# Linear attention in front of two feed-forward layers: the attention part rebuilt on row halves and column tiles of TensorE

## The chip, the cores and the metric

One NeuronCore of a Trainium2 chip runs the whole program. The metric is the device time of one execution in microseconds (us), median over runs. TensorE does the matmuls, VectorE (DVE) and ScalarE (ACT) work on 128 lanes, GpSimd (POOL) multiplies and issues some transfers, SyncE (SP) issues most transfers.

## The reference

Inputs q, k and v have 4 batches, 8 heads, 576 positions and 64 values; w_phi is 64x128. Everything is float32, with weights that arrive as float64.

```
def phi(x):
    proj = x @ w_phi                                   # 128 features
    proj = proj - max(abs(proj), axis=-1)
    return concatenate([exp(proj), exp(-proj)])        # 256 features
q_p, k_p = phi(q), phi(k)
kv, z = k_p.T @ v, sum(k_p over positions)             # 256x64 and 256 per head
x = (q_p @ kv) / (q_p @ z + 1e-6)                      # heads side by side: 2304 x 512
y = (sigmoid(x @ w_gate) * (x @ w_val)) @ w_out        # d_ff 1536
g = y @ w_in;  out = max(0.01 * g, g) @ w_out2         # d_ff 2048
```

## The kernel before

Attention works on 16 pairs of heads: 4 batches times 4 pairs, 128 lanes for the two heads' 64 values. Of the 576 positions 512 are "main" and 64 are the remainder; the remainders of two pairs are worked together. For one pair the steps are: transposes of k and q (`transposed`, tile `ps_t`), projection by a block-diagonal weight `wbd` of 128x256 that serves both heads at once (`proj`, tile `ps_p`), on VectorE the largest absolute value and the subtraction, on ScalarE the two exponentials (`ka`), the sum of features times values (`kv_main`, tile `kv`, 64 output lanes at a time), transposes of the centred q (`q_f`, tile `ps_q`) with their exponentials, and the weighted sums (`num`, tile `ps_n`). The weight of `num` is 128 columns wide: 64 columns are a head's values and one of the others is z, so the denominators come out as one more row of the same matmul. Then `norm1` to `norm3`: a DMA brings the denominator row onto 128 lanes, VectorE inverts it, two DMAs spread it through DRAM, POOL multiplies, and ScalarE and VectorE split the result x into a high part `xh` and a low part `xl`.

The feed-forward layers multiply such high and low parts in a format called float32r: `mm3` (lines 52 to 54) makes three matmuls, high by high, high by low and low by high. Before the change attention does so too in most pairs: `PLAIN_P` and `PLAIN_N` (line 254) name the pairs that use plain float32, 2 of 16 for the projection and 8 of 16 for the weighted sums. A plain float32 matmul stands in the trace as two matmul instructions, a float32r one as one. The split costs a ScalarE cast (line 48) and a VectorE subtraction (line 49; line 433 for the exponentials of q).

The weights are decoded from float64 on VectorE and ScalarE in pieces (`decode`, lines 102 to 114). While attention runs, the three decoded keys of the first feed-forward step are made, in 6 slots, and from pair 4 on `M` pieces put the first feed-forward step of batches 0 to 2 (tiles `pg`, `pv`, `po`) between the pairs. `ORDERS` and `SLOTS` say in which order the pieces of each pair are written; within that, a scheduler orders the instructions on every engine. PSUM has eight banks of 128x512: three shared ones (`at`), two for `kv` and `ps_n`, three for the feed-forward step. After attention come the rest of layer 1 and layer 2 (tile `ps_u` for the first matmul of each, `ps_p` again for the second), which the change does not touch.

Of the kernel before, what the change touches and what calls it, by code (L numbers as in the profile page):

```python
# [9 lines left out]
F32 = mybir.dt.float32  # L10
# [9 lines left out]
def linear_attention_moe(ctx, tc, q, k, v, w_phi, w_gate, w_val, w_out, w_in2, w_out2, out):  # L20
# [9 lines left out]
    NB = B + 1  # L30
    bw = [MAIN] * B + [REM * B]
# [4 lines left out]
    wpa = ctx.enter_context(tc.tile_pool(name="wpa", bufs=1))  # L36
    dr = ctx.enter_context(tc.tile_pool(name="dr", bufs=1, space=bass.MemoryType.DRAM))
# [33 lines left out]
    free = deque((wpa, f"w{i}") for i in range(6))  # L71
# [11 lines left out]
    pools = {}  # L83
# [44 lines left out]
    def first_weights():  # L128

        for i in range(3):  # L130
            _, w, expo = weight(1, 0, i)
            r = {k: take(F32R) for k in ("hi", "lo")}
            raws = [fetch((1, 0, i), j) for j in range(2)]
            yield
            for j, raw in enumerate(raws):
                cs = slice(512 * j, 512 * j + 512)
                m = pools["dec"].tile([128, 512], I32, tag="m", name="m")
                for n, _ in enumerate(decode(raw, m, r["hi"][0][:, cs], r["lo"][0][:, cs], expo)):
                    if n in (2, 4, 5):
                        yield  # L140
            for k in ("hi", "lo"):
                r["v" + k] = r[k][0].rearrange("p (k f) -> p k f", f=w)
            wts[1, 0, i] = r

    def decoded(keys, reserve, hold):
# [4 lines left out]
        for n, key in enumerate(keys):  # L150
# [34 lines left out]
            wts[key] = r  # L185

# [48 lines left out]
    def down1(c, b, h):  # L235
        for e in range(KD):
            po = pools["po"].tile([128, 512], F32, tag="po", name="po")[:, :bw[b]]
            for f in range(CH):
                if f:
                    yield 0  # L240
                mm_down1(po, wts[1, c, 2], b, e, h, f)
            first_sum(b, e, po, pools["tp"].tile([128, 512], F32, tag="st", name="st"))
            yield
# [10 lines left out]
    PLAIN_P, PLAIN_N = {0, 2}, {0, 1, 2, 3, 4, 5, 12, 14}  # L254

    wbd = wk.tile([128, 2 * NF], F32, name="wbd")
    wbh = wk.tile([128, 2 * NF], F32R, name="wbh")
    wbl = wk.tile([128, 2 * NF], F32R, name="wbl")
    nc.vector.memset(wbd, 0.0)

    ps = ps_a.tile([128, 128], F32, tag="at", name="ps_w", bufs=3)
# [13 lines left out]
    kvzs = {}  # L275
    for nm, dts in (("f", (F32,)), ("r", (F32R, F32R))):
        kvzs[nm] = []
        for i in range(1):
            z = [wk.tile([128, 2, 256], dt, name=f"kvz{nm}{i}{j}") for j, dt in enumerate(dts)]
            for t in z:  # L280
                if nm == "f":
                    nc.gpsimd.memset(t[:, :, 65:128], 0.0)
                else:
                    nc.gpsimd.tensor_copy(t[:, :, 65:128], kvzs["f"][i][0][:, :, 65:128])
            kvzs[nm].append(z)

    nat = {}

    def load_pair(b, c):
        for nm, src in (("k", k), ("q", q)):  # L290
            t = ld.tile([128, J, 2, D], F32, tag=nm, name=nm)
            for h in range(2):
                nc.sync.dma_start(out=t[:, :, h], in_=src[b, 2 * c + h, 0:MAIN, :].rearrange("(p j) d -> p j d", j=J))
            nat[nm, b, c] = t
            if (nm, b, c) == ("k", 0, 0):
                for h in range(2):
                    nc.sync.dma_start(out=wbd[64 * h:64 * h + 64, h * NF:(h + 1) * NF], in_=w_phi)
# [9 lines left out]
        vf = nat["v", b, c] = vfs[c % 2]  # L307
        for h in range(2):
            vs = v[b, 2 * c + h]
            nc.sync.dma_start(out=vf[:, 0:J, 65 * h:65 * h + 64], in_=vs[0:MAIN].rearrange("(p j) d -> p j d", j=J))  # L310
            nc.sync.dma_start(out=vf[64 * h:64 * h + 64, J, 66 * h:66 * h + 64], in_=vs[MAIN:S])

    def parts(ps, n, tag, b, c):

        if KD * b + c in PLAIN_P:
            x = xt.tile([128, n], F32, tag=tag + "hi", name=tag + "f")
            nc.scalar.copy(x, ps)
            return (x,)
        hi = xt.tile([128, n], F32R, tag=tag + "hi", name=tag + "hi")
        lo = xt.tile([128, n], F32R, tag=tag + "lo", name=tag + "lo")  # L320
        split(ps, hi, lo)
        return hi, lo

    def transposed(nm, b, c):
        src = nat.pop((nm, b, c))
        ps = ps_a.tile([128, 512], F32, tag="at", name="ps_t", bufs=3)
        for j in range(J):
            nc.tensor.transpose(ps[:, 128 * j:128 * j + 128], src[:, j].rearrange("p h d -> p (h d)"), ident)
        return parts(ps, MAIN, "x", b, c)

    def transposed_rem(nm, b, g):
        src = nat.pop((nm + "r", b, g))
        ps = ps_a.tile([128, 512], F32, tag="at", name="ps_t", bufs=3)
        nc.tensor.transpose(ps[:, 0:128], src.rearrange("p h d -> p (h d)"), ident)
        return parts(ps[:, 0:128], 128, "xr", b, 2 * g)

    def proj(x, c0, n, tag, bufs):

        ps = ps_a.tile([128, 2, 2, NF], F32, tag="at", name="ps_p", bufs=3)
        for i in range(n):  # L340
            l = [p[:, c0 + 128 * i:c0 + 128 * i + 128] for p in x]
            if len(l) == 1:
                nc.tensor.matmul(ps[:, i], l[0], wbd, start=True, stop=True)
            else:
                mm3(ps[:, i], l[0], l[1], wbh, wbl, True, True)
        m = wk.tile([128, 2, 2], F32, tag="m", name="m", bufs=4)
        nc.vector.tensor_reduce(out=m[:, :n], in_=ps[:, :n], axis=AX.X, op=ALU.max, apply_absolute_value=True)
        t = wk.tile([128, n, 2, NF], F32, tag=tag, name=tag, bufs=bufs)
        nc.vector.tensor_tensor(out=t, in0=ps[:, :n], in1=m[:, :n].unsqueeze(3).to_broadcast([128, n, 2, NF]), op=ALU.subtract)
        return t  # L350

    def features(t, n, tag, bufs):

        a = wk.tile([128, n, 2, 2, NF], F32, tag=tag, name=tag, bufs=bufs)
        for s, sc in enumerate((1.0, -1.0)):
            nc.scalar.activation(out=a[:, :, :, s, :], in_=t, func=ACTF.Exp, scale=sc)
        return a
# [6 lines left out]
    def t_k(p):  # L364
        p.kT = transposed("k", p.b, p.c)

    def t_q(p):
        p.qT = transposed("q", p.b, p.c)

    def t_r(p):  # L370
        if p.c % 2 == 0:
            rem["kT"] = transposed_rem("k", p.b, p.c // 2)
            rem["qT"] = transposed_rem("q", p.b, p.c // 2)

    def p_k(p, i):
        p.kf.append(features(proj(p.kT, 256 * i, 2, "t", 4), 2, "ka", 3))

    def p_kr(p):
        if p.c % 2 == 0:
            rem["k"] = features(proj(rem["kT"], 0, 1, "tr", 1), 1, "kar", 1)  # L380

    def p_q(p, i):
        p.tq.append(proj(p.qT, 256 * i, 2, "tq", 2))

    def p_qr(p):
        if p.c % 2 == 0:
            rem["q"] = proj(rem["qT"], 0, 1, "tqr", 1)

    def kv_main(p, s):

        ps = ps_a.tile([128, 2, 65], F32, tag=f"kv{s}", name="kv")
        vf = nat["v", p.b, p.c]
        cols = [slice(64 * i, 64 * i + 64) for i in range(2)]
        for j in range(J):
            for h in range(2):
                for cs in cols:
                    nc.tensor.matmul(ps[cs, h], p.kf[j // 2][:, j % 2, h, s, cs], vf[:, j, 64 * h:64 * h + 65], start=(h, j) == (0, 0), stop=False)
        for cs in cols:
            nc.tensor.matmul(ps[cs].rearrange("p h w -> p (h w)"), rem["k"][:, 0, p.c % 2, s, cs], vf[:, J], start=False, stop=True)
# [652 lines left out]
```

## Time and profile before

| | |
|---|---|
| Median of 3 runs | 1060.35 us (1058.79 to 1060.79) |
| The profiled execution's own time | 1053.95 us |
| Its span, first to last instruction | 1052.1 us |
| TensorE matmul busy | 1011.1 us, 96% |
| TensorE weight load busy | 843.9 us, 80% |
| VectorE busy | 778.9 us, 74% |
| ScalarE busy | 521.0 us, 50% |
| GpSimd busy | 169.7 us, 16% |
| Granted TensorE clock, mean | 0.995 |

Busy time counts a matmul from its start to a modelled end, and matmuls overlap, so a busy TensorE can still have room. How fast it works is read from the distance between the starts of successive matmuls.

### The profile page before, as it was taken

How to read it: one execution, taken by the hardware profiler on the slowest of the kernel's cores; microseconds unless marked ns; L12 is line 12 of the kernel's file. 1: busy time of each engine (PE TensorE's matmuls, PEld its weight loads, DVE VectorE, ACT ScalarE, POOL GpSimd, SP SyncE). 2: the span in 40 equal slices, each digit the busy share in tenths (PEclk: the TensorE clock that was granted, in tenths of full speed). 3: DMA queues.
4: the chain of work that ended last, by engine and by line, in shares of the span. 5: the costliest groups of instructions: out<-in, count | busy, mean ns of one | idle time of the engine just before them, and what ended most of it. 6: DMA issues, size and time to landing. Idle time of an engine off the chain costs nothing.

```text
span 1052.1 us, 16161 instructions
## 1 busy us (share of the span) xinstructions
PE 1011.1 (96%) x5986; PEld 843.9 (80%) x5986; DVE 778.9 (74%) x1373; ACT 521.0 (50%) x1066; POOL 169.7 (16%) x217
## 2 busy tenths in 40 slices
PE   7898999999999899999999999899999999999998
PEld 5677878788788788888888878688888888888886
DVE  4974877877389758395784969998797887979555
ACT  4666676767455545354454434487343343533221
POOL 0112121212201123324143120001010010101000
PEclk9999999999999999999999999999999999999999
DMA  5643344342298988769399494536172442515143
GB/s 142 156 101 89 95 102 108 79 109 75 69 304 243 314 162 257 96 151 268 62 251 189 88 322 180 179 132 239 41 240 82 159 156 85 183 58 180 43 165 132
DMA packets 119485, 160.13 MB, mean 152 GB/s; under 512 B 68720, under 2 KB 71408, under 8 KB 119408
## 3 DMA queue, kind: packets, MB, share of 16 engines
q1 hardware_dynamic: 95216, 94.09, 29.0%
q0 software_dynamic: 24192, 65.02, 24.4%
q8 instruction: 47, 0.77, 0.3%
q14 instruction: 30, 0.25, 0.1%
HBM read 109.64 MB, written 49.36 MB: 151 GB/s over the span
## 4 chain that ended last, share of the span: by engine, by line
PE 56%; DVE 6%; issue 5%; DMA 3%; POOL 2%; ACT 0%; POOLq 0%; ACTq 0%; DVEq 0%
PE ps_u L53 10%; PE ps_u L54 10%; PE ps_u L52 10%; PE ps_p L52 9%; PE ps_p L53 9%; PE ps_p L54 9%; POOL accd L682 2%; DVE acc L742 1%; DMA raw<-in_moe_w_gate_dram 1%; DVE w L753 1%; DMA w<-td 1%; DVE w L114 1%; DMA raw<-in_moe_w_out_dram 1%; POOL w L794 0%; DVE m L107 0%
## 5 line engine op out<-in xcount | busy, mean ns | idle before, releaser
L834 DVE TENSOR_TENSOR q<-ps_u,q 128x512 f32<-128x512 f32 x160 | 109.6, 686 | 66.6 <-PE ps_u L54 60.6
L52 PE MATMUL ps_u<-xh,w 128*128 128x512 f32 (+1 forms) x432 | 151.6, 352 | 1.6 <-ACT xh L48 1.5
L53 PE MATMUL ps_u<-xl,w 128*128 128x512 f32 (+1 forms) x432 | 152.1, 352 | 0.4 <-DVE xl L49 0.2
L54 PE MATMUL ps_u<-xh,w 128*128 128x512 f32 (+1 forms) x432 | 151.4, 351 | 0.0
L904 DVE TENSOR_TENSOR acc<-acc,ps_p 128x512 f32<-128x512 f32 x126 | 86.2, 684 | 39.5 <-PE ps_p L54 39.0
L52 PE MATMUL ps_p<-w,gh 128*128 128x512 f32 x288 | 112.2, 390 | 0.0
L53 PE MATMUL ps_p<-w,gh 128*128 128x512 f32 x288 | 112.0, 389 | 0.0
L54 PE MATMUL ps_p<-w,gl 128*128 128x512 f32 x288 | 111.8, 389 | 0.0
L794 POOL DMA_DIRECT2D w<-td x88 | 48.7, 563 | 379.9 <-PE ps_u L54 365.4
L682 POOL DMA_DIRECT2D accd<-w x80 | 70.7, 888 | 227.8 <-ACT w L681 141.9
L52 PE MATMUL ps_u<-w 128*128 128x512 f32 x256 | 100.1, 391 | 0.8 <-DVE q L834 0.8
L53 PE MATMUL ps_u<-w 128*128 128x512 f32 x256 | 100.0, 390 | 0.7 <-DMA w<-td 0.7
L54 PE MATMUL ps_u<-w 128*128 128x512 f32 x256 | 99.6, 389 | 0.0
L52 PEld LDWEIGHTS ps_u<-xh,w 128*128 128x128 f32 x432 | 82.2, 191 | 13.6 <-ACT xh L48 1.9
L53 PEld LDWEIGHTS ps_u<-xl,w 128*128 128x128 f32 x432 | 82.4, 191 | 12.3 <-DVE xl L689 0.6
L54 PEld LDWEIGHTS ps_u<-xh,w 128*128 128x128 f32 x432 | 82.2, 190 | 10.8
L470 POOL TENSOR_TENSOR rb<-u,rb 64x576 f32<-64x576 f32 x32 | 48.9, 1527 | 233.2 <-DMA rb<-rd 82.7
L52 PE MATMUL ps_p<-gh,w 128*128 128x512 f32 (+1 forms) x216 | 79.0, 370 | 7.6 <-DVE acc L685 4.1
L720 ACT ACTIVATE q<-q 128x512 f32<-128x512 f32 x48 | 30.2, 632 | 112.2 <-DVE q L834 112.1
L53 PE MATMUL ps_p<-gl,w 128*128 128x512 f32 (+1 forms) x216 | 79.8, 370 | 0.7 <-DVE gl L49 0.6
L54 PE MATMUL ps_p<-gh,w 128*128 128x512 f32 (+1 forms) x216 | 79.4, 369 | 0.0
L49 DVE TENSOR_TENSOR gl<-q,gh 128x512 fp32r<-128x512 f32 (+1 forms) x102 | 61.7, 613 | 19.3 <-ACT gh L48 19.1
(151 smaller groups left out, 2248.0 us busy)
## 6 DMA issues: line engine op xcount, KB each, us to landing
w<-td POOLq DMA_DIRECT2D x88, 512.0 KB, 6.1
td<-w SPq DMA_DIRECT2D x32, 512.0 KB, 3.3
accd<-w POOLq DMA_DIRECT2D x64, 256.0 KB, 6.1
raw<-in_moe_w_out_dram SPq DMA_DIRECT2D x28, 512.0 KB, 4.5
raw<-in_moe_w_in_dram SPq DMA_DIRECT2D x16, 512.0 KB, 4.2
raw<-in_moe_w_gate_dram SPq DMA_DIRECT2D x12, 512.0 KB, 5.4
raw<-in_moe_w_val_dram SPq DMA_DIRECT2D x12, 512.0 KB, 5.8
rb<-rd SPq DMA_DIRECT2D x32, 144.0 KB, 3.1
```

Source lines behind the costliest of these rows:

```text
L49: nc.vector.tensor_tensor(out=lo, in0=src, in1=hi.bitcast(F32), op=ALU.subtract)
L52: nc.tensor.matmul(ps, lh, rh, start=first, stop=False, **kw)
L53: nc.tensor.matmul(ps, lh, rl, start=False, stop=False, **kw)
L54: nc.tensor.matmul(ps, ll, rh, start=False, stop=last, **kw)
L114: nc.vector.tensor_tensor(out=lo, in0=mf, in1=hi.bitcast(F32), op=ALU.subtract)
L470: nc.gpsimd.tensor_tensor(out=p.rb[sl], in0=p.u[h][sl], in1=p.rb[sl], op=ALU.mult)
L682: nc.gpsimd.dma_start(out=accd[b][:, e], in_=st, accum_op=ALU.add)
L720: nc.scalar.activation(out=th, in_=t, func=ACTF.Lrelu)
L742: nc.vector.tensor_tensor(out=o, in0=x, in1=y, op=ALU.subtract)
L794: nc.gpsimd.dma_start(out=ts[n][k][0].bitcast(F32), in_=td[l, pair, n][:, k])
L834: nc.vector.tensor_tensor(out=o, in0=x, in1=y, op=ALU.add)
L904: nc.vector.tensor_tensor(out=a, in0=a, in1=po, op=ALU.add)
```

## The change

- The projection reads one head's 64 lanes and writes its 128 features: a matmul on a row half of TensorE (64 of 128 rows), 8 for k and 8 for q of a pair, with head 0 and head 1 in turn, each head into its own bank of a double bank (`pair_bank`, 128x2x512).
- The weighted sums write 64 lanes per head (column tiles of 64), 8 matmuls of 288 columns; the denominators are 8 matmuls of their own whose weight is z, repeated over 32 columns, in four column tiles of 32 (`den`, tile `ps_d`). VectorE copies them to `dd`.
- All of it is plain float32 in all 16 pairs; the splits of q, k, their exponentials and kv are gone.
- VectorE and ScalarE take a double bank at once: 1024 columns for projections, transposes and exponentials, 576 for the copy of the sums. PSUM now has two double banks (`pp`), two single ones (`at`) and two for the feed-forward step (`pg`, `pv`, which also take `po`).
- k, q and v of a pair come by one DMA for both heads; the first q is issued by ScalarE and w_phi by GpSimd.
- The order has 19 lists, one for each step, whose pieces may belong to a pair of up to 4 steps before; a `manual_schedule` makes TensorE follow the written order in this stage. There are 10 slots for decoded weights in attention instead of 6, and decoding uses the general stream there.

```diff
-    free = deque((wpa, f"w{i}") for i in range(6))
+    free = deque((wpa, f"w{i}") for i in range(NWA))        # NWA = 10
...
-    PLAIN_P, PLAIN_N = {0, 2}, {0, 1, 2, 3, 4, 5, 12, 14}
+    def pair_bank(name):
+        return ps_a.tile([128, 2, 512], F32, tag="pp", name=name, bufs=2)
+    def one_bank(w, name):
+        return ps_a.tile([128, 512], F32, tag="at", name=name, bufs=2)[:, :w]
...
+    def proj(x, tag):
+        ps = pair_bank("ps_p")
+        for j in range(J):
+            for h in range(2):
+                rows = slice(64 * h, 64 * h + 64)
+                nc.tensor.matmul(ps[:, h, 128 * j:128 * j + 128], x[rows, 128 * j:128 * j + 128], wbd[rows, h * NF:(h + 1) * NF], start=True, stop=True)
+        return centred(ps.rearrange("p h (j f) -> p (h j) f", j=J), [2 * J, NF], tag, 1)
...
+    def num(p):
+        ps = pair_bank("ps_n")
+        for s in range(2):
+            for n in range(2):
+                for h in range(2):
+                    nc.tensor.matmul(ps[COLS[h], n, 0:288], p.kvz[:, s, h, h:h + 64], p.qf[s][:, h, HALF[n]], start=s == 0, stop=s == 1)
+        p.u = wk.tile([128, 2, 288], F32, tag="u", name="u", bufs=2)
+        nc.scalar.copy(p.u, ps[:, :, 0:288])
+    def den(p):
+        ps = one_bank(288, "ps_d")
+        for s in range(2):
+            for h in range(2):
+                z = p.kvz[:, s, h, 64 * (1 - h):64 * (1 - h) + 1].to_broadcast([128, 32])
+                for n in range(2):
+                    i = 2 * h + n
+                    nc.tensor.matmul(ps[32 * i:32 * i + 32], z, p.qf[s][:, h, HALF[n]], start=s == 0, stop=s == 1)
+        p.dd = wk.tile([128, 288], F32, tag="dd", name="dd", bufs=2)
+        nc.vector.tensor_copy(p.dd, ps)
...
-        "tk tq nn0 nn1 nn2 tr pk0 M nm3 nn3 nm1 pkr pk1 nm2 pq0 pqr M pq1 qr M qf0 M M qf1 kv0 M ld kv1",
+        "n1:qf tt n1:kv ld pk n1:nn M d M n1:dn pq n2:nm3 n1:nm1 kv n1:nm2 M",
...
+    with tc.manual_schedule(engines={mybir.EngineType.PE}):
```

The first place is TensorE in the middle of the stage. Before, these are a pair's last weighted sums, the next pair's projection and the start of its feature sums (`wbh`, `wbl`: high and low part of the projection weight; `kvzr`: parts of kv and z; 64x65 is a column tile; x16 counts matmuls as written):

```order
L52 MATMUL ps_n<-qh,kvzr_140 128x288
L53 MATMUL ps_n<-ql,kvzr_140 128x288
L54 MATMUL ps_n<-qh,kvzr_141 128x288
L52 MATMUL ps_p<-wbh,xhi 128x256
L53 MATMUL ps_p<-wbl,xhi 128x256
L54 MATMUL ps_p<-wbh,xlo 128x256
...
L397 MATMUL kv<-vf_133,ka 64x65 x8
L410 MATMUL ps_r<-ident,tqr 128x128
L397 MATMUL kv<-vf_133,ka 64x65 x8
L399 MATMUL kv<-vf_133,kar 64x130 x2
L397 MATMUL kv<-vf_133,ka 64x65
```

Now, the feature sums of a pair, the projection of the next one, weighted sums, a piece of the feed-forward step, and denominators:

```order
L387 MATMUL kv<-vf_129,ka 64x65 x16
L389 MATMUL kv<-vf_129,kar 64x130 x2
L387 MATMUL kv<-vf_129,ka 64x65 x16
L389 MATMUL kv<-vf_129,kar 64x130 x2
L348 MATMUL ps_p<-wbd,x 128x128 x8
L415 MATMUL ps_n<-qf,kvz 64x288 x8
L54 MATMUL pg<-xh_81,w 128x512
L55 MATMUL pg<-xl_82,w 128x512
...
L426 MATMUL ps_d<-qf,kvz 32x288 x8
```

Three float32r matmuls of full width have become row halves of 128 columns, column tiles of 64 for the sums, and new column tiles of 32. TensorE's mode (full array, row half, column tile of 64 or of 32) changes 125 times up to the first `ps_u` in this order, and 84 times in the order of before.

The second place is VectorE over about one pair, before (`ql`: low part of the exponentials of q, `xlo`: low part of the transposed k and q):

```order
L49 TENSOR_TENSOR kvzr_141<-kv,kvzr_140 128x2x65
L433 TENSOR_TENSOR ql<-qa,qh 128x576 x2
L49 TENSOR_TENSOR kvzr_141<-kv,kvzr_140 128x2x65
L433 TENSOR_TENSOR ql<-qa,qh 128x576 x2
L49 TENSOR_TENSOR xlo<-ps_t,xhi 128x512 x2
L49 TENSOR_TENSOR xrlo<-ps_t,xrhi 128x128
L49 TENSOR_TENSOR xl_87<-rb,xh_86 128x512
L49 TENSOR_TENSOR xrlo<-ps_t,xrhi 128x128
L347 TENSOR_REDUCE m<-ps_p 128x4
L49 TENSOR_TENSOR xl_95<-rb,xh_94 128x64
L349 TENSOR_TENSOR t<-ps_p,m 128x512
L347 TENSOR_REDUCE m<-ps_p 128x2
```

and now (`dd`: copy of the denominators; `gl`: low part of the feed-forward hidden value):

```order
L51 TENSOR_TENSOR gl<-th,gh 128x512
L337 TENSOR_REDUCE m<-ps_p 128x8
L51 TENSOR_TENSOR xl_92<-rb,xh_91 128x512
L339 TENSOR_TENSOR t<-ps_p,m 128x1024
L337 TENSOR_REDUCE m<-ps_p 128x8
L428 COPY dd<-ps_d 128x288
L339 TENSOR_TENSOR tq<-ps_p,m 128x1024
```

The subtractions for `kvzr`, `ql`, `xlo` and `xrlo` are gone, each pair of 512-wide rows is one of 1024, and the copy `dd` is new.

## Rows read from the trace of the kernel before

**Rows 1.** Busy time by stretch: from:to, length, engines, TensorE clock, DMA share, GB/s.
```profile
7.10:279.30 272.20, 249.37 (x2367) 205.95 (x2368) 192.34 (x357) 178.73 (x477) 46.02 (x30) 0.99 0.40 102
279.30:400.00 120.70, 114.80 (x560) 95.44 (x559) 89.12 (x154) 61.40 (x106) 19.83 (x21) 0.99 0.83 242
400.00:600.00 200.00, 200.00 (x983) 169.63 (x982) 139.63 (x252) 94.13 (x167) 62.78 (x80) 1.00 0.75 169
```

**Rows 2.** One tile's matmuls: count, duration min/median/max, first to last start.
```profile
L52 PE MATMUL ps_u<-xh,w x432: 277/389/513, 279.3 to 1036.5; 128*128 128x512 f32 x90, 128*128 128x256 f32 x54
L54 PE MATMUL po<-gh,w x24: 387/389/480, 136.8 to 290.6; 128*128 128x512 f32 x24
```

**Rows 3.** Groups by line and shape to 420 us: count, busy us, mean ns, idle before.
```profile
L397 PE MATMUL kv<-vf,ka 128*64 128x65 f32 x1024 | 40.8, 225 | 1.6 <-ACT u L451 1.0 <-ACT ka L356 0.6
L448 PE MATMUL ps_n<-qf,kvzf 128*128 128x288 f32 x128 | 38.7, 421 | 4.2 <-ACT qf L419 4.1
L52 PE MATMUL ps_p<-wbh,xhi 128*128 128x256 f32 x112 | 34.4, 307 | 1.1 <-DVE xl L49 1.1
L52 PE MATMUL ps_n<-qh,kvzr 128*128 128x288 f32 x64 | 19.9, 313 | 0.0
L343 PE MATMUL ps_p<-wbd,xf 128*128 128x256 f32 x32 | 8.5, 398 | 3.0 <-ACT xf L317 1.6 <-DVE tr L349 1.4
```

**Rows 4.** Timeline of TensorE, first two pairs: start us, us, instruction.
```profile
7.14 0.63 PE L328 MATMUL ps_t<-ident,q 128*128 128x128 f32 x4 [1.18 <-DMA q<-in_q_dram]
7.61 0.60 PE L328 MATMUL ps_t<-ident,k 128*128 128x128 f32 x4
...
30.54 0.28 PE L52 MATMUL ps_p<-wbh,xhi 128*128 128x256 f32 x1
...
31.50 0.28 PE L54 MATMUL ps_p<-wbh,xlo 128*128 128x256 f32 x1
31.70 0.69 PE L397 MATMUL kv<-vf,ka 128*64 128x65 f32 x16
...
33.32 1.10 PE L397 MATMUL kv<-vf,ka 128*64 128x65 f32 x32
34.25 0.39 PE L399 MATMUL kv<-vf,kar 128*64 128x130 f32 x4
34.58 1.36 PE L416 MATMUL ps_q<-ident,tq 128*128 128x128 f32 x8
...
43.41 1.62 PE L448 MATMUL ps_n<-qf,kvzf 128*128 128x288 f32 x6
44.87 0.60 PE L328 MATMUL ps_t<-ident,q 128*128 128x128 f32 x4
```

**Rows 5.** Timeline of TensorE around 209 and 345 us.
```profile
209.30 0.29 PE L52 MATMUL ps_n<-qh,kvzr 128*128 128x288 f32 x1
209.43 0.29 PE L53 MATMUL ps_n<-ql,kvzr 128*128 128x288 f32 x1
...
345.00 0.39 PE L52 MATMUL ps_u<-xh,w 128*128 128x512 f32 x1
...
346.13 0.39 PE L54 MATMUL ps_u<-xh,w 128*128 128x512 f32 x1
```

**Rows 6.** Waits of TensorE up to 280 us: total us, times, longest.
```profile
PE ps_n L448 <- ACT qf L419: 4.1, 2, 3.4
...
PE ps_n L53 <- DVE ql L433: 2.5, 3, 1.1
```

**Rows 7.** Groups on VectorE and ScalarE by shape to 420 us, as rows 3.
```profile
L347 DVE TENSOR_REDUCE m<-ps_p 128x4 f32<-128x512 f32 x64 | 43.4, 683 | 7.9 <-PE ps_p L343 4.1 <-PE ps_p L54 3.3
L433 DVE TENSOR_TENSOR ql<-qa,qh 128x576 fp32r<-128x576 f32 x32 | 33.3, 1054 | 15.2 <-ACT qa L419 9.0 <-ACT qa L420 6.1
L451 ACT COPY u<-ps_n 128x288 f32<-128x288 f32 x64 | 26.4, 426 | 15.1 <-PE ps_n L54 7.8 <-PE ps_n L448 7.1
L742 DVE TENSOR_TENSOR acc<-acc 128x1024 f32<-128x1024 f32 x8 | 9.8, 1219 | 5.7 <-DMA acc<-xd 5.7
```

More of the change, by code (lines that the diff above doesn't have):

```diff
@@ L185, in decoded, with ahead, need @@
             wts[key] = r
+    reserve = [0]
+    hold = [(3, 0)]
+    order = [(1, c, i) for c in range(NC1) for i in range(3)] + [(2, c, i) for c in range(NC2) for i in (0, 2)]
+    stream = decoded(order, reserve, hold)
+    side = []
+    def ahead(n):
+        for _ in range(n):
+            if side and next(side[0], None) is None:
+                side.pop(0)
+            if not next(stream, None) and not side:
+                break
+    def need(*key):
+        while key not in wts:
+            if next(stream, None) is not True and key not in wts:
+                raise RuntimeError(f"no room for {key}: {len(free)} slots free")
     def drop_sums(*key):
@@ L331, in transposed_rem @@
[L331 to L357, printed above, removed]
+            nc.sync.dma_start(out=vf[64 * h:64 * h + 64, J, 66 * h:66 * h + 64], in_=v[b, 2 * c + h, MAIN:S])
     class Pair:
@@ new lines, in kv_main, with q_f @@
+        p.kvz = wk.tile([128, 2, 2, 65], F32, tag="kvz", name="kvz", bufs=2)
+        nc.scalar.copy(p.kvz, ps)
+    def q_f(p):
+        ps = pair_bank("ps_q")
+        for h in range(2):
+            for j in range(J):
+                nc.tensor.transpose(ps[:, h, 128 * j:128 * j + 128], p.tq[:, J * h + j], ident)
+        psr = one_bank(128, "ps_r")
+        nc.tensor.transpose(psr, rem["q"][:, p.c % 2], ident)
+        p.qf = []
+        for sc in (1.0, -1.0):
+            qf = wk.tile([128, 2, S], F32, tag="qf", name="qf", bufs=4)
+            nc.scalar.activation(out=qf[:, :, MAIN:S], in_=psr.rearrange("p (h t) -> p h t", h=2), func=ACTF.Exp, scale=sc)
+            p.qf.append(qf)
+        for qf, sc in zip(p.qf, (1.0, -1.0)):
+            nc.scalar.activation(out=qf[:, :, 0:MAIN], in_=ps, func=ACTF.Exp, scale=sc)
@@ L615, in linear_attention_moe @@
         xs[key] = [(None, (xp, n + tag)) for n in ("xh", "xl")]
-    reserve = [0]
-    hold = [(3, 0)]
-    order = [(1, c, i) for c in range(1, NC1) for i in range(3)] + [(2, c, i) for c in range(NC2) for i in (0, 2)]
-    stream = decoded(order, reserve, hold)
-    side = []
-    def ahead(n):
-        for _ in range(n):
-            if side and next(side[0], None) is None:
-                side.pop(0)
-            if not next(stream, None) and not side:
-                break
-    def need(*key):
-        while key not in wts:
-            if next(stream, None) is not True and key not in wts:
-                raise RuntimeError(f"no room for {key}: {len(free)} slots free")
     pend = deque()
```

299 lines of the change are left out of this document (102 added, 197 removed), and 24 rows, old and new, of the table ORDERS.

## The prediction

> **What bounds the kernel now.** I read the busy time by stretch first. From 400 us on TensorE is busy without a gap (200.00 of 200 us between 400 and 600), while VectorE and ScalarE have room; up to 279.3 us it is busy for 249.37 of 272.20 us [rows 1]. So the program is bound by TensorE, and the attention stage is where it is both busy with work that can shrink and at times waiting. The stage ends where the first `ps_u` starts, at 279.3 us; the last `po` matmuls of the feed-forward step that runs beside attention come as late as 290.6 us [rows 2].
>
> Busy time does not tell how fast TensorE works, since matmuls overlap, so the second view is the timeline, where I take the distance between starts. Prices of one matmul instruction in an undisturbed stream: float32r of 256 columns (31.50 − 30.54)/8 = 0.12 us; plain float32 of 288 columns (44.87 − 43.41)/6 = 0.243 us; column tiles of 64 with 65 columns (34.25 − 33.32)/32 = 0.029 us; a transpose (7.61 − 7.14)/4 = 0.12 us [rows 4]; float32r of 288 columns 0.13 us and of 512 columns (346.13 − 345.00)/5 = 0.226 us [rows 5]. A plain matmul is two instructions: `ps_n` on line 448 is written 64 times and counts 128 [rows 3]. So plain float32 is no cheaper than float32r at the same shape: 2 x 0.243 = 0.49 us against 3 x 0.13 = 0.39 us at 288 columns. What can win is the halves and tiles. For that the `kv` rows are the evidence: at full width 65 columns of plain float32 would take 0.243 x 65/288 = 0.055 us an instruction, and they take 0.029: two column tiles of 64 work at the same time.
>
> **The sum of the stage before.** `kv` 1024 x 0.029 = 29.7 [rows 3, 4] and 128 of the 130-column kind at (0.33 − 0.08)/4 = 0.0625 = 8.0 [rows 4], where 0.08 is a mode change (below); 288 transposes 33.8; projections in float32r 3 x 112 plus 36 for the remainders at 0.12 = 44.6; plain ones 32 + 8 at 0.243 x 256/288 = 0.216 = 8.6; weighted sums 128 x 0.243 = 31.1 and 3 x 64 x 0.13 = 25.0 [rows 3]; the feed-forward step 216 x 0.226 = 48.8. Between a matmul of the full array and a `kv` one 0.20 us pass instead of 0.12 (31.50 to 31.70 [rows 4]): 0.08 for a mode change, 84 times, 6.7. Together 236.3 us. The stage lasts 272.2 us, and 21 of the 216 feed-forward matmuls (4.7 us) come after its end. So 272.2 + 4.7 − 236.3 = 40.6 us are lost to waits and start-up.
>
> **The change part by part.**
>
> *Projection.* 256 matmuls on row halves, 512 instructions of 128 columns. Alone each costs 0.243 x 128/288 = 0.108. No row before shows row halves; the bounds are one after another (55.3 us) and two at once (27.6 us). I take two at once: the nearest row is that of the column tiles in `kv`, which run so, and the two heads alternate. The remainders keep full width, now all plain: 32 x 0.216 = 6.9. Together 34.5 instead of 53.2.
>
> *Weighted sums and denominators.* The sums: 256 instructions at 0.243, two column tiles at once, as `kv` shows: 31.1; one after another would be 62.2. The denominators were free before, one more row of the same output; now they are 256 more instructions of 288 columns in four tiles of 32. Four at once they take 15.6, two at once 31.1, one by one 62.2. I take four, since the `kv` rows show that a tile doesn't wait for its neighbour, and keep 31.1 as the upper end. Together 46.7 instead of 56.1.
> Here a page speaks against the full factor: the Trainium skill, "TensorE: Matmul & The Clock Gate", Part 3, measured 2.38 times for three column tiles, not three. The `kv` rows agree (0.055/0.029 = 1.9, not 2). By that the four tiles would give some 3.2 and the denominators 19.6 us, an estimate from that page, 4 us above my term.
>
> *Mode changes.* 125 in the written order now, 84 before: 10.0 instead of 6.7.
>
> *Unchanged on TensorE:* `kv`, transposes, feed-forward, 120.3. The sum after is 120.3 + 34.5 + 46.7 + 10.0 = 211.5 us, 24.8 less than before.
>
> *Other engines.* VectorE (192.34 us in the stage) and ScalarE (178.73) [rows 1] get lighter. VectorE loses all of `ql`, 33.3; 64 rows of 0.683 for the maximum become 32 of about 1.22 (the 1024-wide row), 4 less, and the same again for the subtraction; new is `dd`, 16 times about 0.43, the time of the like copy `u` on ScalarE: 6.8 [rows 7]. ScalarE loses the casts and the second set of exponentials of q, and copies `u` in 16 wide pieces instead of 64. Neither decides then. Two more keys of weights are decoded in the stage on VectorE; that is work taken from the stretch behind it.
>
> *Transfers.* k, q, v and the denominators take fewer issues on SP. The first transposes start at 7.14 us after a wait for a DMA [rows 4]; now they wait for the remainders, issued as fifth on SP, where q was sixth. I count nothing; the rest of the start-up is the same chain.
>
> *Lost time.* TensorE's waits for `ql` (2.5 us) go with their cause; the wait for the exponentials of q (4.1) stays, as these are still one ScalarE pass after the transposes [rows 6]. Against that, TensorE now follows the written order: a matmul that waits holds up all behind it, the feed-forward pieces too, where the scheduler's order mixed them in one by one. Lower end 12 us (start-up and little more), upper end the 41 of now. I take 25, near the middle: the other engines are lighter, and in most steps a feed-forward piece or another pair's piece stands between a matmul and what it needs.
>
> *Behind the stage.* TensorE is busy for 114.80 of 120.70 us up to 400, with DMA engines at 0.83 [rows 1]. Decoding further ahead could give back up to 6 us there, or transfers crowded by an earlier end could cost as much. I take nothing.
>
> **The sum.** The gain is 24.8 + (40.6 − 25) = 40.4 us. The profiled execution's own time was 1053.95 (span 1052.1), so 1013.6 for such a one. The timed runs had a median of 1060.35, 6.4 more; on their scale it is 1020.
>
> **Rivals.**
>
> *The written order costs more than it saves (slower).* A double bank is held from its first matmul until VectorE or ScalarE has read it to the end, 1024 columns at about 1.22 us a pass [rows 7], two passes after a projection. There are two such banks and five fillings for each pair, 80 in all, and TensorE may not go round a filling that waits. If each exposes 1.0 us, 80 us are lost, the stage is 80 + 211.5 − 276.9 = 15 us longer, and the run takes 1075. It decides from (40.6 + 24.8)/80 = 0.82 us for each filling. For it: the first four pairs have no feed-forward pieces between them. Against it: in the later pairs about 4 us of such pieces stand between (48.8 over 11 steps), and the other engines have lost work. The Trainium skill, "TensorEngine Tiling (Array Packing)", PSUM Bottleneck, warns of this: tiles speed up TensorE, not the emptying of PSUM.
>
> *The halves or tiles don't work at the same time* (the change doesn't do what it says). 27.7 + 31.1 + 46.6 = 105 us more, less the 40 gained: 1125. Against it: the `kv` rows [rows 3, 4].
>
> *Only a small gain.* Denominators two at once (15.5 more) and the lost time stays at 41: gain 9, 1051. Or half of the gain is given back behind the stage, where TensorE waits for weights or sums: 1040. For it: DMA share 0.83 there [rows 1]. Against it: what waits there was ready no later before.
>
> *A larger gain.* Lost time 12 and 6 us back behind the stage: gain 24.8 + 28.6 + 6 = 59, 1001.
>
> **How the numbers follow.** The forecast with its surroundings (1003 to 1036) has 0.55. The small gain (1036 to 1058) has 0.23; the large gain, at or below 1001, has 0.04, and 0.01 lies between it and the forecast. The written order 0.12, no overlap 0.02, and 0.03 within 0.2% of now, about 2 us, which is what a measurement of this kernel can tell from no change. Faster has 0.83, same 0.03, slower 0.14. A range from 1001 to 1055 leaves out the slower cases, the same and the edge below, about 0.2; the likeliest case's own is 1003 to 1036.
>
> **What would show it.** The first `ps_u` should start at about 243 us (7.1 + 211.5 + 25). The starts of `ps_p` should lie 0.054 us apart in the mean, those of `ps_n` 0.12, those of `ps_d` 0.06 (0.12 if two at once). Around a change of mode 0.08 us more. TensorE's waits in the stage should be on ScalarE's exponentials and on `t`, not on `dd` or `u`. VectorE and ScalarE in the stage should be below 170 us each. I am wrong if a tile's rows lie a full 0.108 or 0.243 apart, if the stage ends after 270 us, or if it ends early and the stretch up to 400 us shows TensorE waiting longer than the 6 us of now.

## The result and the profile after

| | before | after |
|---|---|---|
| Median (range), us | 1059.57 (1058.40 to 1060.79), 4 runs | 1018.20 (1015.95 to 1020.80), 4 runs |
| The profiled execution's own time | 1053.95 | 1018.86 |
| Its span | 1052.1 | 1017.1 |
| First `ps_u` | 279.3 | 256.3 |
| From there to the end | 772.8 | 760.8 |
| TensorE, VectorE, ScalarE busy | 1011.1, 778.9, 521.0 | 981.9, 723.4, 475.3 |

The ratio is 0.961, 95% interval 0.9583 to 0.9637. The medians differ by 41.4 us, the profiled executions by 35.1: the one of before ran at a mean granted clock of 0.995, while 34 other executions of it had 0.985 to 0.995 and spans of 1050.4 (at 0.995) to 1060.5 us (at 0.986). So some 6 of the 41.4 us are not in the two traces.

Busy time by stretch, cut as [rows 1], now at 256.3 us, and the stage once more in two parts; the last two rows are the same two parts in the kernel before:

```profile
7.10:256.30 249.20, 226.96 (x2712) 167.57 (x2713) 156.81 (x260) 143.58 (x245) 21.80 (x15) 0.99 0.50 131
256.30:400.00 143.70, 142.86 (x727) 121.63 (x725) 88.29 (x148) 65.92 (x115) 32.71 (x39) 1.00 0.82 221
7.10:100.00 92.90, 76.11 (x1002) 56.66 (x1002) 80.12 (x137) 60.14 (x102) 7.33 (x5) 0.98 0.68 176
100.00:256.30 156.30, 150.84 (x1712) 110.91 (x1711) 76.70 (x124) 83.44 (x144) 14.47 (x10) 1.00 0.39 104
7.10:100.00 92.90, 79.12 (x723) 62.01 (x725) 65.47 (x124) 55.47 (x139) 11.90 (x8) 0.98 0.50 126
100.00:279.30 179.30, 170.25 (x1648) 143.93 (x1649) 126.87 (x234) 123.26 (x339) 34.12 (x22) 1.00 0.35 89
```

TensorE still stands idle for 22.2 us of the stage (22.8 before), 16.8 of them in its first 93 us, where VectorE is busy for 80.1. There both grew, from 13.8 and 65.5 us; part of it are the further keys of weights, decoded in this stretch. From 100 us on the idle time fell from 9.1 to 5.5. Behind the stage only 0.8 us of idle time are left up to 400 us, where there were 5.9. VectorE and ScalarE have 156.8 and 143.6 us in the stage, below the 170 forecast.

The tiles that mark the end of the stage, as [rows 2]: no feed-forward matmul of the stage is left over behind the first `ps_u` any more.

```profile
L54 PE MATMUL ps_u<-xh,w x432: 277/389/505, 256.3 to 1001.3; 128*128 128x512 f32 x90, 128*128 128x256 f32 x54
L54 PE MATMUL po<-gh,w x24: 392/399/503, 128.8 to 255.6; 128*128 128x512 f32 x24
```

TensorE's groups up to 420 us, as [rows 3]. Row halves show as 64*128 and column tiles of 32 as 128*32. The busy time of one says nothing of the rate, since the tiles overlap:

```profile
L348 PE MATMUL ps_p<-wbd,x 64*128 64x128 f32 x512 | 36.7, 284 | 5.0 <-ACT x L323 2.3 <-DVE t L339 1.9 <-ACT qf L406 0.8
L426 PE MATMUL ps_d<-qf,kvz 128*32 128x288 f32 x256 | 18.8, 412 | 2.5 <-ACT kvz L391 1.6 <-DVE tr L339 0.8
```

The rate is in the timeline, as [rows 4]: start, length, instruction, at 126 and 188 us.

```profile
126.59 1.16 PE L348 MATMUL ps_p<-wbd,x 64*128 64x128 f32 x16
127.68 1.18 PE L426 MATMUL ps_d<-qf,kvz 128*32 128x288 f32 x16
128.79 0.50 PE L54 MATMUL po<-gh,w 128*128 128x512 f32 x1
...
129.68 2.16 PE L415 MATMUL ps_n<-qf,kvz 128*64 128x288 f32 x16
131.77 0.50 PE L54 MATMUL po<-gh,w 128*128 128x512 f32 x1
...
188.66 2.06 PE L348 MATMUL ps_p<-wbd,x 64*128 64x128 f32 x32
190.65 1.18 PE L426 MATMUL ps_d<-qf,kvz 128*32 128x288 f32 x16
```

From start to start a block takes 1.09 us (projection), 1.11 (denominators) and 2.09 (sums), the change of mode at its end included. Two projection blocks in a row take 1.99, so 16 more instructions cost 0.90, 0.056 each: two at once. Sixteen denominator instructions at 0.243 one after another would be 3.89 us; they take 1.11, so four work at once, 0.061 each and some 0.13 for the change. Within a block of denominators four of them start 7 ns apart, every 0.245 us.

TensorE's waits up to 250 us, as [rows 6]: of the two old entries `ql` is gone, and `qf` has 0.8 us (the row of `ps_p` above). What stands there is short and spread.

```profile
PE ps_t L318 <- issue: 3.3, 2, 2.2
PE ps_p L348 <- ACT x L323: 2.3, 5, 1.2
PE ps_n L415 <- DVE t L339: 2.0, 1, 2.0
PE ps_t L318 <- ACT u L417: 1.8, 2, 1.3
```

VectorE's and ScalarE's new groups, as [rows 7]: the passes over a double bank of 1024 take 1.22 us and `dd` 0.45, as estimated.

```profile
L337 DVE TENSOR_REDUCE m<-ps_p 128x8 f32<-128x1024 f32 x32 | 39.0, 1218 | 34.0 <-PE ps_p L348 34.0
L428 DVE COPY dd<-ps_d 128x288 f32<-128x288 f32 x16 | 7.2, 450 | 0.5 <-PE ps_d L426 0.5
```

### The profile page after: what moved, and what is told of

Same layout as the page of the kernel before. It is cut to its first block, busy times and chain, and to the rows that moved or that the text cites. A ratio compares the mean times of both kernels' runs of the same rounds, so it can differ in the third digit from the quotient of the medians.

```text
span 1017.1 us, 16194 instructions
## 1 busy us (share of the span) xinstructions
PE 981.9 (97%) x6310; PEld 801.8 (79%) x6310; DVE 723.4 (71%) x1236; ACT 475.3 (47%) x817; POOL 144.7 (14%) x200
## 4 chain that ended last, share of the span: by engine, by line
PE 81%; DVE 7%; DMA 6%; ACT 2%; issue 1%; POOL 1%; SPq 1%; POOLq 0%; ACTq 0%; DVEq 0%
PE ps_u L55 13%; PE ps_u L54 13%; PE ps_u L56 13%; PE ps_p L54 10%; PE ps_p L55 10%; PE ps_p L56 10%; PE ps_p L348 2%; DMA rb<-rd 2%; PE kv L387 2%; PE ps_n L415 2%; DVE m L337 1%; DMA rd<-r 1%; POOL rb L443 1%; PE ps_t L318 1%; DMA w<-td 1%
## 5 line engine op out<-in xcount | busy, mean ns | idle before, releaser
L56 PE MATMUL ps_u<-w 128*128 128x512 f32 x256 | 99.7, 390 | 0.0
L610 ACT COPY w<-ps_p 128x512 f32<-128x512 f32 (+1 forms) x80 | 43.3, 543 | 54.3 <-PE ps_p L56 47.7
```

The costliest lines, as they stand in the source:

```text
L56: nc.tensor.matmul(ps, ll, rh, start=False, stop=last, **kw)
L610: nc.scalar.copy(st, po)
```

## The experiments

All but one edit the kernel after; the times are medians, the ratios are to the kernel before, run on the same chip. "Stage" is the start of the first `ps_u` in the profiled execution (256.3 in the kernel after).

| run | median us | ratio, 95% | stage |
|---|---|---|---|
| e6_plain: before, all plain | 1069.14 | 1.0111 (1.0074 to 1.0147) | 287.8 |
| e3_fullproj: no row halves | 1030.42 | 0.9736 (0.9706 to 0.9765) | 265.5 |
| e4_numrow: tiles not in turn | 1027.68 | 0.971 (0.9686 to 0.9734) | 265.5 |
| e5_den2: denominators twice | 1038.58 | 0.981 (0.9787 to 0.9833) | 271.8 |
| e2_sched: no written order | 1021.89 | 0.966 (0.9625 to 0.9694) | 256.1 |
| e11_onepair: one double bank | 1120.78 | 1.0586 (1.0535 to 1.0637) | 356.0 |
| e1_slots6: 6 slots | 1022.83 | 0.9662 (0.964 to 0.9684) | 253.7 |
| e7_spread: decoding moved | 1023.16 | 0.9666 (0.9635 to 0.9696) | 256.8 |
| e9_nodecode: no decoding | 1022.93 | 0.9675 (0.9632 to 0.9717) | 258.2 |
| e10_bufs6: more buffers | 1023.87 | 0.9679 (0.9643 to 0.9715) | 253.6 |
| e12_xsplit: x copied in two | 1029.02 | 0.9704 (0.966 to 0.9748) | 263.0 |
| e13_nonorm: no way through DRAM | 1016.58 | 0.9625 (0.9596 to 0.9654) | 250.3 |

**Is it the plain format?** e6_plain is the kernel before with every pair plain:

```diff
-    PLAIN_P, PLAIN_N = {0, 2}, {0, 1, 2, 3, 4, 5, 12, 14}
+    PLAIN_P, PLAIN_N = set(range(16)), set(range(16))
```

> The kernel before with plain float32 in all 16 pairs (one line), so with the changed kernel's arithmetic but full-width matmuls, two of 8 and 16 instructions where float32r has three: no halves, no tiles. Theory: plain float32 alone adds 14 x 0.58 us in the projections, 12 x 0.07 in the remainders and 8 x 0.77 in the weighted sums, 15 us of stream; VectorE loses its subtractions (some 60 us) and with them some 4 us of TensorE's waits: 1058 + 11 = 1069 us. Rival: the splits on VectorE and ScalarE were what held the stage, and taking them away is where the change gains: 1045 us or less.

It came out as expected, 1069.14: the format alone costs. TensorE's stage got longer by 8.5 us, though VectorE's busy time in it fell from the 192.34 of [rows 1] to 137.07:

```profile
7.10:287.80 280.70, 260.79 (x2180) 206.46 (x2181) 137.07 (x269) 160.51 (x413) 42.44 (x30) 0.99 0.39 100
```

**Do the halves and tiles work at once?** Three edits to the kernel after:

```diff
 e3_fullproj
-                rows = slice(64 * h, 64 * h + 64)
+                rows = slice(0, 128)
 e4_numrow (and for s in the third place)
-        for s in range(2):
+        for h in range(2):
 e5_den2
-        for s in range(2):
+        for s in (0, 1, 0, 1):
```

> The changed kernel with the 16 projection matmuls of a pair on all 128 rows of TensorE (the other head's rows of the weight are zero, so the sums are the same) instead of row halves. Theory: row halves work two at a time, so their rows lie 0.059 us apart and will lie 0.109 apart; 512 x 0.05 = 25.6 us more stream, less some 5 us for mode changes that fall away, and TensorE's stream sets the length: 1018 + 20 = 1038 us, with the first ps_u near 276 us. Rival: the stage is set by the chain through VectorE and ScalarE, with 36 us of waits on TensorE that can take up more stream: then the time rises by under 10 us, below 1028.

> The changed kernel with the weighted sums written head by head, so that all matmuls of one column tile stand together instead of alternating between the two tiles; same matmuls, same result. Theory: two column tiles work at the same time only where they alternate in the written order; in the new order a pair's 16 instructions take 16 x 0.243 = 3.9 us instead of 1.95, 31 us more in all, of which up to 4 us hide in waits: 1018 + 28 = 1046 us. Rival 1: TensorE takes up the other tile's matmuls from further down its queue: no change, 1018. Rival 2: the stream doesn't set the length: under 10 us more.

> The changed kernel with each pair's denominators worked out twice (the second time over the first, same result). Theory: four column tiles of 32 at once, 16 more instructions in 4 x 0.245 = 1.0 us a pair, 16 us in all, and the stream sets the length, with the mode unchanged between the two: 1018 + 14 = 1032 us. Rival: waits take it up, since VectorE's copy of the denominators is not what TensorE waits for: under 5 us more, below 1023.

The same blocks in their timelines, of e3_fullproj, of e4_numrow and of e5_den2:

```profile
127.67 1.95 PE L348 MATMUL ps_p<-wbd,x 128*128 128x128 f32 x16
129.55 1.18 PE L426 MATMUL ps_d<-qf,kvz 128*32 128x288 f32 x16
```

```profile
131.35 3.18 PE L415 MATMUL ps_n<-qf,kvz 128*64 128x288 f32 x16
134.46 0.50 PE L54 MATMUL po<-gh,w 128*128 128x512 f32 x1
```

```profile
133.84 2.15 PE L426 MATMUL ps_d<-qf,kvz 128*32 128x288 f32 x32
135.92 0.50 PE L54 MATMUL po<-gh,w 128*128 128x512 f32 x1
```

At full width the projection block takes 1.88 us instead of 1.09: the row halves do work two at a time. Twice the denominators take 2.08 instead of 1.11, so 16 more cost 0.97, 0.061 each: four at a time. With the sums ordered by tile the block takes 3.11 us, not the 4.05 of one after another (16 x 0.245 + 0.13) nor the 2.09 of two at once: four of eight in each tile still find a partner. The single starts show it: in 14 of the 16 blocks the second tile's first matmul starts 1.03 us into the block, together with the first tile's fifth and ahead of three that are written before it.

Not all of it reaches the time. e3_fullproj came out between its theory and its rival, e4_numrow where its second rival had it, e5_den2 above both. In e3_fullproj 32 blocks x 0.79 = 25 us of stream were added, and the time rose by 12; e4_numrow added 16 and rose by 9.5. TensorE's idle time in the stage shows where most of the rest went: 7.8 + 2.7 = 10.5 us in e3_fullproj, against 22.2.

```profile
7.10:100.00 92.90, 85.07 (x1002) 67.04 (x1002) 81.62 (x138) 60.91 (x103) 7.67 (x5) 1.00 0.69 178
100.00:265.50 165.50, 162.83 (x1713) 127.17 (x1711) 75.67 (x123) 82.94 (x142) 14.13 (x10) 1.00 0.36 98
```

Slower matmuls filled waits that were there anyway. So a faster block is worth about half of its stream time here. e5_den2 is the exception: its stage is longer by all of the 15.5 us of stream, and the time by 20.4. Of that 4.4 lie behind the stage, which is no more than this stretch differs by from one run to another (below).

**Does the written order cost or save?** e2_sched lets the scheduler order TensorE as before; e11_onepair leaves one double bank:

```diff
 e2_sched
-    with tc.manual_schedule(engines={mybir.EngineType.PE}):
+    if True:
 e11_onepair
-        return ps_a.tile([128, 2, 512], F32, tag="pp", name=name, bufs=2)
+        return ps_a.tile([128, 2, 512], F32, tag="pp", name=name, bufs=1)
```

> The changed kernel without the fixed order of TensorE: the scheduler orders its instructions as it does for the other engines, from the same lists of pieces. Theory: the written order makes TensorE stand behind a waiting matmul, but the scheduler is not better at it: the stream is the same 213 us, the lost time 36 plus or minus 10 us: 1008 to 1028 us, first ps_u between 246 and 266. Rival 1: the written order is what keeps the lost time small, and the scheduler puts pieces in front that wait longer, with more changes of mode: over 1030 us. Rival 2: the written order is the main cause of the lost time: under 1008 us.

> One double bank instead of two. Reading a filling out takes about 1.2 us for x, 2.4 for each projection, 2.4 for the exponentials of q and 0.65 for u: 9.1 us a pair, 146 us in 16 pairs. Theory: two double banks are what hides these passes; with one, some 95 us of TensorE's other work in the stage (feed-forward 49, kv 38, denominators 12) can stand beside them where the order allows, so 50 to 110 us are lost: 1070 to 1130 us. Rival (the passes are hidden by what other pieces need anyway, banks decide little): below 1038 us.

The written order neither gains nor costs much: without it the stage ends at the same place, and the two ratios' intervals overlap. It is not without effect. The stage of e2_sched (first row) has 16.7 us of TensorE's idle time instead of 22.2, but 5.3 us more of busy time, at a mean granted clock of 0.98 instead of 0.99. The second double bank is worth 100 us: the stage ends at 356.0, and 80 fillings for 99.7 us are 1.25 us each. The stage of e11_onepair (second row), and TensorE's longest waits up to 365 us:

```profile
7.10:256.10 249.00, 232.28 (x2712) 170.37 (x2712) 155.57 (x260) 144.21 (x245) 21.60 (x15) 0.98 0.50 131
7.10:356.20 349.10, 263.23 (x2713) 190.60 (x2714) 158.44 (x260) 146.02 (x246) 21.10 (x15) 0.87 0.36 94
```

```profile
PE ps_p L348 <- ACT qf L406: 18.2, 9, 2.6
PE ps_n L415 <- DVE tq L339: 12.7, 6, 3.1
PE ps_n L415 <- DVE t L339: 10.7, 4, 5.2
```

Each of these waits is for a pass that reads the one double bank out. TensorE is idle for 85.9 us, 64 more than before this edit. The other 36 us are busy time of the same matmuls, in a stage whose mean granted clock is 0.87 instead of 0.99.

**What gave 7 us behind the stage?** e1_slots6 takes four of the ten slots for decoded weights away:

```diff
-    NWA = 10
+    NWA = 6
```

> The changed kernel with 6 slots for decoded weights in attention instead of 10, so that three keys of weights are decoded there instead of five. Theory: the 7 us that the changed kernel gained behind the stage come from decoding further ahead, and the two further keys (VectorE busy 44.5 of 50 us between 50 and 100 us) cost waits in the stage. Then the first ps_u starts some 3 us earlier than 256.3 us and the stretch behind it is 5 to 8 us longer: about 1021 us against 1018. Rival: the gain behind the stage has nothing to do with the decoding (the result of attention simply arrives in a better order): the stretch behind the stage stays at 761 us and the time is 1018 or, with a lighter VectorE, 1015.

It came out so: 4.6 us slower by the medians, with the stage 2.6 us shorter and the rest 6.1 us longer. TensorE's idle time up to 400 us is back, 4.4 us instead of 0.8, and with it 2.9 us of wait for ScalarE's copy of a feed-forward partial sum out of its bank, which the kernel before has too (3.1 us, its line 681) and the one after has not:

```profile
253.70:400.00 146.30, 141.91 (x718) 120.34 (x717) 99.61 (x171) 70.07 (x123) 32.29 (x38) 1.00 0.85 230
```

```profile
PE ps_p L54 <- ACT w L610: 2.9, 1, 2.9
```

So 3.6 of the 6.1 us are shown at their place. e10_bufs6, which has six slots too, has 4.5 us of idle time there, and the other runs with ten slots 0.5 to 2.5: what decoding ahead is worth there is some 2 to 4 us. The rest behind the stage took 760.8 to 767.1 us in the profiled executions with ten slots, so the remainder is within what differs from one execution to the next.

**What are the idle 22 us of the stage?** Five tries. Decoding on VectorE in front of bank reads: e7_spread takes eight decoding pieces out of the fifth list, e9_nodecode decodes nothing in attention (constants stand for the weights, by two ScalarE copies a half).

```diff
 e7_spread
-        "... n2:nm3 M d n1:dn d d d d n1:nn n1:nm1 d n1:nm2 d d",
+        "... n2:nm3 M n1:dn n1:nn n1:nm1 n1:nm2",
 e9_nodecode (of the first five keys)
-                for _ in decode(raws.popleft(), m[:, cs], hi[:, cs], lo[:, cs], expo):
+                    for o in (hi[:, cs], lo[:, cs]):
+                        nc.scalar.copy(o, one)
```

> The changed kernel with the eight decoding pieces behind the first feed-forward piece in step 4 taken out, so that the same work is taken up in steps 5 to 10, where VectorE is busy for 24 to 28 of 50 us instead of 44.5. Theory: VectorE's decoding delays the projections' subtraction, on which a double bank waits, so lost time between 50 and 100 us falls by 2 to 4 us and the kernel takes 1014 to 1016 us. Rival: the lost time there comes from the written order and ScalarE; no change, 1018.

> The changed kernel with the decoding of the five keys of weights in attention left out: two ScalarE copies of a constant column stand for the two ScalarE passes of each half key, and VectorE does nothing for them (the result is not the reference's). Theory: in the first five pairs the double banks are held by projections whose maximum and subtraction stand behind decoding on VectorE; without it the lost time of the stage falls from 36 to 24 us or less and the first ps_u starts at 246 us or before: 1008 us or less. Rival: the lost time is the chain from transposes over ScalarE's exponentials to the sums in the written order; the first ps_u starts within 4 us of 256.3, 1014 to 1020 us.

Both theories fell. e7_spread ends the stage at 256.8 us, and what it is slower by lies behind the stage (767.1 us instead of 760.8), which neither side expected. e9_nodecode's stage is within its rival's 4 us. Without decoding VectorE is busy for 50.9 us of the first 92.9 instead of 80.1, and TensorE's idle time is 18.2 instead of 16.8 (first row). With six slots (e1_slots6, second row) VectorE has 72.4 us there and TensorE's idle time is 14.0, so what VectorE's decoding costs in this stretch isn't settled:

```profile
7.10:100.00 92.90, 74.71 (x968) 55.22 (x967) 50.90 (x79) 54.89 (x94) 7.06 (x5) 0.96 0.69 188
7.10:100.00 92.90, 78.92 (x1009) 58.42 (x1010) 72.43 (x120) 57.09 (x96) 7.05 (x5) 0.96 0.65 168
```

Then single buffers, and the length of a pair's chain:

```diff
 e10_bufs6 (with NWA = 6)
-        p.x = xt.tile([128, 2, MAIN], F32, tag="x", name="x", bufs=1)
+        p.x = xt.tile([128, 2, MAIN], F32, tag="x", name="x", bufs=2)
-        return centred(ps.rearrange("p h (j f) -> p (h j) f", j=J), [2 * J, NF], tag, 1)
+        return centred(ps.rearrange("p h (j f) -> p (h j) f", j=J), [2 * J, NF], tag, 2)
 e12_xsplit
-            nc.scalar.copy(p.x, ps)
+        for i in range(2):
+            nc.scalar.copy(p.x[:, i], ps[:, i])
```

> Six slots for decoded weights as in e1_slots6 (1022.8 us, first ps_u at 253.7), and with the room x, t and tq each get two buffers. Theory A (the lost time comes from double banks that stay full because the one buffer that they are read out to is still in use, as before ps_t at 29 us): first ps_u 6 to 10 us earlier, at 244 to 248, and 1012 to 1017 us. Theory B (the lost time is the length of the chain from one piece of a pair to its next, each piece waiting for the pass that makes its operand): within 3 us of e1_slots6 in both.

> The copy of x in two of 512 columns, the half of k first, so that pk can start some 0.6 to 1.2 us earlier; ScalarE does 16 copies more, some 3 us. Theory B (chain length is the lost time): the waits of ps_p for x, 2.3 us, mostly go and the stage is 2 to 6 us shorter, 1012 to 1016 us. Rival (what is won in one wait is lost in the next): 1016 to 1021 us and the same first ps_u within 2 us.

More buffers change nothing: e10_bufs6 agrees with e1_slots6 in stage and time. The split copy, meant to shorten a chain, made the stage 6.7 us longer, which neither side expected. Its trace shows the largest wait in the open, at 147 us: start, length, instruction, and in brackets the idle time ahead of it.

```profile
143.40 1.16 PE L346 MATMUL ps_p<-wbd,x 64*128 64x128 f32 x16
...
146.88 1.41 POOL L441 TENSOR_TENSOR rb<-u,rb 128x576 f32<-128x576 f32 x1 [14.62 <-DMA rb<-rd]
...
148.31 0.76 ACT L50 CAST xh<-rb 128x512 fp32r<-128x512 f32 x2 [3.51 <-POOL rb L441]
148.96 0.69 DVE L51 TENSOR_TENSOR xl<-rb,xh 128x512 fp32r<-128x512 f32 x1 [7.03 <-ACT xh L50]
...
149.57 1.22 DVE L335 TENSOR_REDUCE m<-ps_p 128x8 f32<-128x1024 f32 x1
...
151.07 1.22 DVE L337 TENSOR_TENSOR tq<-ps_p,m 128x1024 f32<-128x1024 f32 x1
...
152.39 1.09 PE L318 MATMUL ps_t<-ident,k 128*128 128x128 f32 x4 [3.73 <-issue]
```

Read it from the top: a projection fills its bank by 144.6 us. The spread reciprocals of an earlier pair land late, GpSimd multiplies, ScalarE casts, and VectorE stands 7.03 us before `xl`. Behind `xl` in its queue are the two passes that empty that bank; 0.1 us after the second, TensorE can begin the transposes that need the bank. The wait names no releaser ("issue"); only VectorE's queue, followed back, shows it. And it is paid twice, by the granted clock (third number from the end of a row) in the 4 us behind it, where the same transposes take 1.09 us instead of 0.60 (at 135.99 us of this trace):

```profile
148.00:152.00 4.00, 0.66 (x6) 0.14 (x2) 3.04 (x4) 1.30 (x3) 0.28 (x1) 1.00 0.17 66
152.00:156.00 4.00, 3.61 (x40) 3.31 (x42) 0.81 (x4) 1.35 (x3) 0.00 (x0) 0.57 0.24 54
156.00:160.00 4.00, 4.00 (x76) 3.54 (x73) 0.07 (x1) 1.66 (x5) 0.00 (x0) 1.00 0.64 141
```

From that came the last theory, and e13_nonorm, which takes the transfers of the denominators and their reciprocals away:

```diff
-        nc.sync.dma_start(out=p.d, in_=p.dd[0:128:32, :])
+        nc.vector.tensor_scalar_add(p.d, p.dd[:, 0:9], 1e-6)
...
-        nc.sync.dma_start(out=rd.rearrange("h (p e) -> (h p) e", e=9), in_=r)
-        for h in range(2):
-            nc.sync.dma_start(out=p.rb[64 * h:64 * h + 64], in_=rd[h:h + 1, :].to_broadcast([64, S]))
-        nc.gpsimd.tensor_tensor(out=p.rb, in0=p.u.rearrange("p n t -> p (n t)"), in1=p.rb, op=ALU.mult)
+        nc.gpsimd.tensor_tensor(out=p.rb, in0=uu, in1=uu, op=ALU.mult)
```

> The denominators no longer go through DRAM: no d<-dd, rd<-r and rb<-rd transfers; GpSimd multiplies u by itself instead of by the spread reciprocals, so the normalised values are wrong numbers and the output isn't the reference's. Matmuls, copies, reductions and their order on TensorE stay. In the changed kernel ScalarE stands 23.1 us before the cast xh that waits for GpSimd's product, VectorE 20.8 us behind that cast and 12.8 us before d, all with bank reads queued behind them. Theory C (the lost time is these queues: a bank is read late because its reader waits for the reciprocals' way through DRAM): first ps_u at 240 to 250, 1002 to 1012 us. Theory B (the chain inside each pair, which has no transfer in it): first ps_u at 253 to 259, 1015 to 1022 us.

The stage is 6.0 us shorter, at the edge of what the theory said, while the time, 1016.58, lies where the rival had it; by the ratios it can't be told from the kernel after. The windows part it:

```profile
7.10:100.00 92.90, 78.08 (x1015) 58.87 (x1016) 85.12 (x148) 62.22 (x106) 7.64 (x6) 0.98 0.68 177
100.00:250.30 150.30, 147.99 (x1699) 108.89 (x1698) 71.16 (x113) 81.33 (x140) 11.47 (x10) 1.00 0.30 78
```

From 100 us on, idle time falls from 5.5 to 2.3 us; in the first stretch from 16.8 to 14.8. So the way of the reciprocals through DRAM explains about 5 of the 22 us, by one execution each. Of the 17 that stay, 15 lie in the first 93 us, where the first feed-forward pieces come only at 66 us and every pair waits for its own x, `t` and `kvz`; only slower matmuls covered some of them (e3_fullproj), and no run filled this stretch with other work. That they are this chain is argued, not shown. No version here beats the kernel after clear of noise. No run takes back the wide passes of 1024 columns or the loads by one DMA alone, so what these two parts of the change are worth stays open.

## Why the prediction came out right, point by point

- **The forecast was 1020 (range 1001 to 1055); the median is 1018.2.** That it came so close is partly luck. The gain of 40.4 us between profiled executions came out as 35.0, so the profiled execution took 1018.86 us and not 1013.6. The 6.4 us between before's profiled execution and its median, which the sum was moved by, did not return either: the profiled execution of after is 0.7 above its own median. The two errors, +5.3 and −7.1 us, nearly cancel. As shown above, the profiled execution of before ran at the top of its clock.
- **Stream, −24.8 forecast.** By blocks: projection 32 x 1.09, sums 16 x 2.09, denominators 16 x 1.11, together 86.1 us, against 27.6 + 31.1 + 15.6 and 64 changes at 0.08, 79.4. So 6.7 less was won, 18.1. The rates were right (0.056 forecast 0.054, 0.061 forecast 0.061); the step that was too small is the mode change, 0.13 behind column tiles and 1.09 − 0.90 = 0.19 behind row halves instead of 0.08. The price was read at one place, from start to start across the change, and there it holds (0.09 now). But the second step of the new block is late too: in a projection block it comes 0.21 us after the first, where the later ones take 0.11. The 2.38 times for three column tiles of the Trainium skill, "TensorE: Matmul & The Clock Gate", Part 3, is not the bound here: four tiles in the stream gave the whole factor, 0.243/0.061 = 4. No run has three.
- **Lost time, 40.6 to 25.** The same subtraction gives 249.2 − (211.5 + 6.7) = 31.0. This term was mis-sized too, 9.6 won instead of 15.6, and the changes of mode behind other blocks still stand at 0.08 in it. The windows say more: TensorE's idle time hardly moved (22.8 to 22.2). The reason given, "the other engines are lighter", isn't borne out: up to 100 us VectorE got heavier and the idle time grew, from 13.8 to 16.8. Lighter again, VectorE left 14.0 us in e1_slots6 and 18.2 in e9_nodecode. What fell is time in which TensorE was counted busy beyond the stream's price, 40.6 − 22.8 = 17.8 to 31.0 − 22.2 = 8.8; what that was before isn't settled.
- **Behind the stage, 0 (bound 6 either way).** The effective end before was 279.3 + 4.7 = 284.0, so the rest took 768.1 us, and takes 760.8: 7.3 won. The larger gain's mechanism, decoding further ahead, was right, as e1_slots6 shows for 2 to 4 us. The misses, −12.7 in the stage and +7.3 behind it, partly cancel: 40.4 became 18.1 + 9.6 + 7.3 = 35.0.
- **The first `ps_u` at 243, it came at 256.3,** by the same 12.7 us. The named waits (`qf`, `t`) are there, but small: `qf`, whose 4.1 us were to stay, has 0.8. Beside them stand `x`, `kvz` and bank reads, among them `u` with 1.8 us, which was ruled out.
- **The slower rival** put its price at 1.0 us for each of 80 fillings. That is what one double bank costs (1.25 us, e11_onepair); with two most of it is hidden, and the written order adds nothing to the time (e2_sched). The Trainium skill, "TensorEngine Tiling (Array Packing)", PSUM Bottleneck, warns that reading PSUM out may become the limit when tiles speed TensorE up: the trace agrees where there is one double bank (85.9 us idle), and not where there are two (22.2, as much as before).
- **"Doesn't do what it says"** is ruled out by e3_fullproj, e4_numrow and e5_den2.

## What to carry to other kernels

Price a tiled matmul by the distance from block to block, its mode change included, and order the tiles in turn: the same instructions ordered by tile lost half of the overlap. A faster block on an engine that also waits gives back only part of its time (half in e3_fullproj), so count idle time in the stretch before and after, not only the stream. Give the fillings of PSUM a second bank first: here it was worth more than any other part that was taken back. And follow a wait without a releaser through the in-order queue of the engine that reads the bank: what stood in front of it here was another pair's DMA.

## What the runs showed of the hardware that was not expected

- Four column tiles of 32 start 7 ns apart and run at the full factor of four, in plain float32: 0.061 us for 288 columns against 0.243.
- Matmuls of another column tile begin ahead of their turn: with the sums ordered by tile, the ninth as written starts with the fifth, and a pair takes 3.11 us, between 2.09 and 4.05.
- A wait of a few us can cost twice. After TensorE stood for 3.73 us the granted clock of the next 4 us was 0.57 of full speed, near the lower level of 1.2 GHz, and it was back at 1.00 in the 4 us after that; in e11_onepair, idle for 85.9 of 349.1 us, the whole stage had 0.87. The length of a wait alone does not tell: after waits of 2.50 and 2.75 us (at 49 and 59 us in e9_nodecode) the clock stayed at 1.00, and after one of 2.23 us (at 29 us in the kernel after) it had 0.68 in the next 4 us.
- The time from one execution to the next goes loosely with the mean granted clock: e12_xsplit had spans of 1026.9 to 1029.4 us at 0.988 and 1020.0 at 0.992, but e7_spread's shortest, 1016.9, was at 0.992, and at 0.993 it took up to 1023.9.
